# Attention followed by a SwiGLU block: batch-1 loads behind the casts of batch 0, transposes ahead of the second score burst, and the x of a batch read half a step later

## Chip, cores and metric

The kernel runs on one core of one Trainium2 chip. The metric is the device time of one execution in microseconds (us), as the median of several runs; lower is better.

## What is computed

The input is q, k, v of shape (8, 8, 576, 64) in fp32 (batch, heads, rows, width), 16 beacon rows of k and v per head that stand ahead of the others, and three weights of a gated block. Cut to its core, the reference is:

```
k_all = concatenate([beacon_k, k], axis=2);  v_all = concatenate([beacon_v, v], axis=2)
scores = (1 / sqrt(D)) * q @ k_all^T          # causal among the 576 rows, beacons always seen
a = softmax(scores);  attn = a @ v_all        # (8, 8, 576, 64)
x = attn.transpose(0, 2, 1, 3).reshape(4608, 512)
g = x @ w_gate;  val = x @ w_val              # 512 -> 1536
out = (g * sigmoid(g) * val) @ w_out          # 1536 -> 512, fp32
```

## The kernel before

The recording order is written by hand: instructions stand on each engine in the order in which the text calls them, and an engine takes them in that order. Waits are derived from it: an instruction that reads a tile waits for the last write of the same region that stands ahead of it in the text, and a write waits for the reads ahead of it.

**Attention** goes by batch b and head pair m (4 pairs). For a pair, `cast_k` and `cast_q` (L167 to L178) turn the fp32 tiles `k32` and `q32` into bf16 (`kb`, `qb`), `transpose_k` and `transpose_q` (L180 to L192) transpose them on TensorE into a PSUM tile `t_ps`, which VectorE copies to `kT` and `qT`. `scores1` and `scores2` (L215 to L254) are the two score bursts of a pair: matmuls into two PSUM tiles `s_ps`, Exp on ScalarE into the tiles `p`, causal masks with `affine_select` on GpSimd (L238, two behind the first burst, four behind the second), and then the next group of `pool_todo`: DMA issues on GpSimd's queue for v, the weights, and the k and q of batch 2 onwards. `pv(b, m, hh)` (L258) multiplies with v for one head into `pv_ps` and VectorE normalises into `x` (L274, L275).

**The gated block** goes by chunks of 512 tokens. `G()` runs one unit: eight matmuls of 512 columns (L307), a Tanh (L316) and two VectorE passes (L318, L321) that leave one of the 12 slices of `hT`. `gq` is the queue of units. `F(n)` takes n matmuls of `out_steps` (L326) from the queue `fq`; 12 of them fill one output tile, which VectorE copies out (L345) and SyncE's queue stores. The input `xT` of batch 0 comes from TensorE transposes (`x_transpose_pair`, L282); that of batches 1 to 7 from DMA transposes of `x`, five per batch, on SyncE's queue (`x_transpose`, L290 to L295). A chunk ends at a multiple of 512, a batch at a multiple of 576, so the units of chunk b-1 need the first few of the five blocks of batch b-1.

PSUM: `big` has three buffers (score tiles and units share them), `att` and `outp` have one each. `att` holds in turn `pv_ps`, `xt_ps` and, from batch 1 on, `t_ps`.

**The start** (L374 to L382): SyncE's and ScalarE's queues load k32 and q32 of batch 0, pair by pair. Behind them, on SyncE's queue, stand the 24 loads of batch 1 into the same tiles (L377), in the text ahead of every cast. So the casts of batch 0 wait for those loads too, and read what they left: the scores of batch 0 are computed from the q and k of batch 1.

**Batch 0** (L401 to L417) does for each pair: `scores1`, the first half of the previous pair's `pv`, `scores2`, the second half, an x transpose, then casts and transposes of the next pair (`prep`), all of which stand behind the second burst.

**Steps from batch 1 on** (L430 to L471): a step is one pair. From batch 2 on it has three units: one ahead of `scores1`, one behind `scores2`, one at the end; in batch 1 two. In the step m == 1 the units of chunk b-1 are put into `gq` behind `scores2` and ahead of the second unit:

```python
        if m == 1 and b > 1:
            gq += [(b - 1, f) for f in range(NF)]
            fq += out_steps(b - 2, one_bank)
        if units:
            G()
        if prev:
            pv(*prev, 1)
        F(6)
        if m == 0 and b > 1:
            x_transpose(b - 1)
        if units > 1:
            G()
```

So `x_transpose` is issued at the end of step m == 0, and its result is first read by the second unit of step m == 1.

Of the kernel before, what the change touches and what calls it, by code (L numbers as in the profile page):

```python
# [24 lines left out]
NPE = 3  # L25
# [21 lines left out]
def kernel(  # L47
# [12 lines left out]
    nc = tc.nc  # L60
# [6 lines left out]
    NF = DFF // P  # L67
# [12 lines left out]
    att = ctx.enter_context(tc.tile_pool(name="att", bufs=1, space=bass.MemoryType.PSUM))  # L80
    outp = ctx.enter_context(tc.tile_pool(name="outp", bufs=1, space=bass.MemoryType.PSUM))
# [20 lines left out]
    def tiles(t):  # L102
        return t[:].rearrange("p (c h d) -> p c h d", c=NKT, h=H)
# [14 lines left out]
    def load_q_f32(eng, b, h0, h1):  # L118
        spans(eng, tiles(q32), q, b, h0, h1, 0, 4, 0)
        rows(eng, tiles(q32), q, b, h0, h1, 4, 0, 512, 64)  # L120

    def load_k_f32(eng, b, h0, h1):
        d = tiles(k32)
        rows(eng, d, beacon_k, b, h0, h1, 0, 0, 0, NB)
        rows(eng, d, k, b, h0, h1, 0, NB, 0, P - NB)
        spans(eng, d, k, b, h0, h1, 1, 4, P - NB)
        rows(eng, d, k, b, h0, h1, 4, 0, 496, 80)
# [39 lines left out]
    def cast_k(b, m):  # L167
        d, t, h = tiles(kb[b % 2]), tiles(k32), slice(2 * m, 2 * m + 2)
        nc.vector.tensor_copy(d[:, 0:4, h, :], t[:, 0:4, h, :])  # L169
        nc.vector.tensor_copy(d[0:80, 4, h, :], t[0:80, 4, h, :])  # L170

    def cast_q(b, m):
        d, t, h = tiles(qb[b % 2]), tiles(q32), slice(2 * m, 2 * m + 2)
        for o, i in ((d[:, 0:4, h, :], t[:, 0:4, h, :]), (d[0:64, 4, h, :], t[0:64, 4, h, :])):
            if b:
                nc.scalar.activation(o, i, ACT.Copy)
            else:
                nc.vector.tensor_copy(o, i)  # L178
# [9 lines left out]
    def transpose_k(b, m, pool, tag):  # L188
        transpose_pair(kT, kb, 80, b, m, pool, tag)

    def transpose_q(b, m, pool, tag):
        transpose_pair(qT, qb, 64, b, m, pool, tag)  # L192

    def prep(b, m):
        cast_k(b, m)
        cast_q(b, m)
        transpose_k(b, m, outp, "outp")
        transpose_q(b, m, outp, "outp")

    def dma_transposes(b):  # L200
        def one(dst, src, c, n):
            nc.sync.dma_start_transpose(
# [47 lines left out]
    def scores1(b, m):  # L250
        scores(b, m, 0, SCORES1, P1_COLS)

    def scores2(b, m):
        scores(b, m, 1, SCORES2, P2_COLS)  # L254
# [27 lines left out]
    def x_transpose_pair(b, m):  # L282
        t_ps = att.tile([P, S], BF16, name="xt_ps", tag="att")
        for c, (q0, n) in enumerate(QBLOCKS):
            nc.tensor.transpose(
                t_ps[:, q0 : q0 + n], xs[b][0:n, c, P * m : P * m + P], ident[0:n, 0:n]
            )
        nc.vector.tensor_copy(xT[:, m, S * b : S * b + S], t_ps[:])
# [63 lines left out]
    gq, fq = [], []  # L352
# [3 lines left out]
    def G():  # L356
        if gq:
            return gv_unit(*gq.pop(0))
# [15 lines left out]
    for h in range(0, H, 2):  # L374
        load_k_f32(nc.sync, 0, h, h + 2)
        load_q_f32(nc.scalar if h < 4 else nc.sync, 0, h, h + 2)
    for h in (0, 4):  # L377
        load_k_f32(nc.sync, 1, h, h + 4)
        load_q_f32(nc.sync, 1, h, h + 4)
    make_identity(nc, ident)  # L380
    for load in v_loads(0, 0, 4) + v_loads(0, 4, 8):
        load()  # L382
# [15 lines left out]
    def after(s):  # L398
        return steps[s + 1] if s + 1 < len(steps) else (B, 0)

    prep(0, 0)  # L401
    last = NPAIR - 1
    for m in range(NPAIR):
        scores1(0, m)
        if m:
            pv(0, m - 1, 0)
        scores2(0, m)
        if m:
            pv(0, m - 1, 1)
        if m >= 2:  # L410
            x_transpose_pair(0, m - 2)
        if m < last:
            prep(0, m + 1)
    x_transpose_pair(0, last - 1)
    pv(0, last, 0)
    pv(0, last, 1)
# [13 lines left out]
    for s in range(NPAIR, len(steps)):  # L430
        b, m = steps[s]
        nxt = after(s)
        units = {NPAIR: 0, NPAIR + 1: 2, NPAIR + 2: 2, NPAIR + 3: 2}.get(s, 3)
        if units > 2:
            G()
        scores1(b, m)
        if nxt[0] == 1:
            cast_k(*nxt)
        if prev:
            pv(*prev, 0)  # L440
        F(6)
        scores2(b, m)
        if nxt[0] == 1:
            cast_q(*nxt)
        if nxt[0] < NPE:
            transpose_k(*nxt, att, "att")
        if m == 1 and b > 1:
            gq += [(b - 1, f) for f in range(NF)]
            fq += out_steps(b - 2, one_bank)
        if units:  # L450
            G()
        if prev:
            pv(*prev, 1)
        F(6)
        if m == 0 and b > 1:
            x_transpose(b - 1)
        if units > 1:
            G()
        if nxt[0] < NPE:
            transpose_q(*nxt, att, "att")  # L460

        if m == 1 and NPE <= b + 1 < B:
            todo = dma_transposes(b + 1)
        for _ in range(4):
            if todo:
                todo.pop(0)()
        if m == 3 and NPE <= b + 2 < B:
            pool_todo += group(k_loads(b + 2, 0, H) + q_loads(b + 2, 0, H), 6)
        if m == 1 and NPE <= b + 1 < B:
            pool_todo += group(v_loads(b + 1, 0, H), 3)  # L470
        prev = (b, m)  # L471
# [51 lines left out]
```

## Time and profile before

| | us |
|---|---|
| median of 3 runs (460.53 to 462.31) | 461.3 |
| the profiled execution | 461.59 |
| its span, first to last instruction | 459.9 |
| TensorE (PE) busy with matmuls | 390.9 (85%) |
| VectorE (DVE) busy | 232.8 |
| ScalarE (ACT) busy | 172.3 |
| GpSimd (POOL) busy, its DMA issues among it | 178.4 |
| mean granted TensorE clock | 0.948 of full speed |

In the rows below, a line of the timeline gives start, length, engine, source line, operation, tile written and tiles read, how many instructions are merged, and in brackets the idle time of the engine ahead of it and what ended it. SPq and ACTq are DMA issues on the queues of SyncE and ScalarE. "PEclk" is the granted clock. The 1.7 us between span and time lie outside the span.

### The profile page before, as it was taken

The page shows a single profiled execution, that of the slowest core. Times are in us where ns is not written, and L with a number is a line of the kernel's source. Part 1 is how long each engine was busy: PE and PEld are TensorE (multiplying, and loading weights), DVE is VectorE, ACT ScalarE, POOL GpSimd, SP SyncE. Part 2 cuts the span into 40 slices and gives each one's busy share as a digit, 9 for nine tenths or more (in the row PEclk, how much of TensorE's full clock was granted, in tenths as well). Part 3 has the DMA queues.
Part 4 walks back from the last instruction along what each step waited for, and adds up shares of the span by engine and source line. Part 5 has one row for each costly group of instructions (what it writes and reads, how often), then busy time and mean ns, then how long its engine had stood idle before and what let it go on. Part 6 is the DMA issues. An engine that isn't in the chain of part 4 may idle for free.

```text
span 459.9 us, 7296 instructions
## 1 busy us (share of the span) xinstructions
PE 390.9 (85%) x2780; PEld 186.1 (40%) x2780; DVE 232.8 (51%) x450; ACT 172.3 (37%) x245; POOL 178.4 (39%) x345
## 2 busy tenths in 40 slices
PE   0056697777799959998999799999999998999996
PEld 0034444343344424443444344444444443444442
DVE  1035444555256525654555365656655664576562
ACT  1034227444344434444444344445455421222220
POOL 7038608765861733456436442646222100000000
PEclk9999578889799979998999899999999999999999
DMA  9969658669999991959497949899221013010002
GB/s 165 173 134 99 73 87 95 45 50 164 140 143 90 88 161 29 132 53 171 66 115 70 178 64 109 73 173 121 42 76 47 23 34 87 26 46 20 27 30 108
DMA packets 169491, 41.70 MB, mean 91 GB/s; under 512 B 159216, under 2 KB 164848, under 8 KB 169456
## 3 DMA queue, kind: packets, MB, share of 16 engines
q0 software_dynamic: 101936, 16.75, 51.1%
q1 hardware_dynamic: 65120, 23.89, 25.9%
q10 hardware_dynamic: 2400, 0.59, 0.6%
q8 instruction: 22, 0.36, 0.3%
q14 instruction: 13, 0.11, 0.1%
HBM read 38.27 MB, written 9.44 MB: 104 GB/s over the span
## 4 chain that ended last, share of the span: by engine, by line
PE 65%; DVE 13%; DMA 9%; ACT 5%; SPq 4%; issue 2%; POOL 1%; DVEq 0%; ACTq 0%
PE gv_ps L307 32%; PE o_ps L336 18%; PE pv_ps L266 7%; PE s_ps L220 7%; DMA xT<-x 5%; DVE u L318 4%; DVE hT L321 4%; ACT th L316 4%; SPq L295 2%; DMA k<-in_k_dram 2%; PE t_ps L185 2%; DMA q<-in_q_dram 2%; DMA vb<-in_v_dram 1%; DVE x L275 1%; SPq L108 1%
## 5 line engine op out<-in xcount | busy, mean ns | idle before, releaser
L318 DVE SCALAR_TENSOR_TENSOR u<-th,gv_ps 128x512 f32<-128x512 f32 x108 | 74.3, 688 | 148.5 <-ACT th L316 147.8
L316 ACT ACTIVATE th<-gv_ps 128x512 f32<-128x512 f32 x108 | 64.5, 597 | 202.9 <-PE gv_ps L307 197.6
L238 POOL TENSOR_SCALAR_AFFINE_SELECT p<-p 128x256 bf16<-128x256 bf16 x192 | 66.7, 379 | 186.2 <-ACT p L229 185.8
L229 ACT ACTIVATE p<-s_ps 128x720 bf16<-128x720 f32 (+1 forms) x128 | 103.7, 868 | 64.6 <-PE s_ps L220 64.4
L307 PE MATMUL gv_ps<-xT,wg 128*128 128x512 bf16 x432 | 117.3, 396 | 9.8 <-DMA xT<-x 9.8
L307 PE MATMUL gv_ps<-xT,wv 128*128 128x512 bf16 x432 | 114.4, 388 | 0.0
L336 PE MATMUL o_ps<-wo,hT 128*128 128x512 bf16 x432 | 105.6, 382 | 2.1 <-DVE o_sb L345 2.1
L321 DVE SCALAR_TENSOR_TENSOR hT<-gv_ps,u 128x512 bf16<-128x512 f32 x108 | 74.7, 691 | 3.7
L307 PEld LDWEIGHTS <-wv 128*128 128x128 bf16 x432 | 43.3, 100 | 54.4 <-issue 6.3
L307 PEld LDWEIGHTS <-wg 128*128 128x128 bf16 x432 | 40.9, 101 | 58.1 <-issue 15.4
L220 PE MATMUL s_ps<-qT,kT 64*128 64x80 bf16 (+5 forms) x384 | 47.7, 308 | 12.1 <-DVE qT L186 7.4
L336 PEld LDWEIGHTS <-hT 128*128 128x128 bf16 x432 | 39.3, 99 | 42.8 <-issue 3.7
L266 PEld LDWEIGHTS <-p 128*128 128x128 bf16 x960 | 39.2, 103 | 25.6 <-issue 15.0
L266 PE MATMUL pv_ps<-vb,p 128*128 128x65 bf16 x960 | 44.9, 203 | 4.0 <-DMA vb<-in_v_dram 2.4
L114 POOL DMA_DIRECT2D vb<-in_v_dram x50 | 39.9, 814 | 0.2 <-issue 0.2
L220 PEld LDWEIGHTS <-kT 64*128 64x128 bf16 x384 | 16.4, 99 | 43.5 <-issue 37.1
L275 DVE TENSOR_TENSOR x<-pv_ps,rec 128x320 bf16<-128x320 f32 x64 | 31.5, 492 | 2.2
L345 DVE COPY o_sb<-o_ps 128x512 f32<-128x512 f32 x36 | 24.8, 689 | 12.6 <-PE o_ps L336 12.1
L114 POOL DMA_DIRECT2D qb<-in_q_dram x35 | 28.6, 853 | 0.0
L185 PE MATMUL t_ps<-ident,kb 128*128 128x128 bf16 (+1 forms) x60 | 7.1, 265 | 25.0 <-DVE kb L169 23.8
L114 POOL DMA_DIRECT2D kb<-in_k_dram x35 | 28.4, 833 | 0.0
L274 DVE RECIPROCAL rec<-pv_ps 128x5 f32<-128x5 f32 x64 | 11.9, 186 | 19.5 <-PE pv_ps L266 19.5
(30 smaller groups left out, 67.0 us busy)
## 6 DMA issues: line engine op xcount, KB each, us to landing
out_dram<-o_sb SPq DMA_DIRECT2D x36, 256.0 KB, 2.2
qb<-in_q_dram POOLq DMA_DIRECT2D x20, 128.0 KB, 5.3
vb<-in_v_dram POOLq DMA_DIRECT2D x18, 128.0 KB, 5.9
kb<-in_k_dram POOLq DMA_DIRECT2D x15, 128.0 KB, 4.1
k<-in_k_dram SPq DMA_DIRECT2D x16, 96.0 KB, 2.8
q<-in_q_dram SPq DMA_DIRECT2D x12, 128.0 KB, 2.8
wg<-in_moe_w_gate_dram POOLq DMA_DIRECT2D x4, 384.0 KB, 5.5
wv<-in_moe_w_val_dram POOLq DMA_DIRECT2D x4, 384.0 KB, 6.7
```

What stands on the lines that cost most here:

```text
L114: eng.dma_start(dst[p0 : p0 + n, c, h0:h1, 0:D], src[b, h0:h1, r : r + n, :].rearrange("h j d -> j h d"))
L220: nc.tensor.matmul(s[hh][:, col : col + n], lhsT=kT[b % 2][r, m, P * t : P * t + P], rhs=qT[b % 2][r, m, q0 : q0 + n], start=True, stop=True,)
L229: nc.scalar.activation(p[:, cols[0] : cols[1]], s[hh][:, cols[0] : cols[1]], ACT.Exp, scale=0.125)
L238: nc.gpsimd.affine_select(out=ap, in_=ap, compare_op=ALU.is_ge, fill=0.0, base=base, pattern=pattern, channel_multiplier=-1,)
L266: nc.tensor.matmul(o_ps[:, c, 0 : D + 1], lhsT=pt[2 * (m % 2) + hh][w][:, col : col + P], rhs=vb[b % 2][:, t, h, 0 : D + 1], start=(t == 0 ...
L275: nc.vector.tensor_tensor(out=xs[b][:, :, D * h : D * h + D], in0=o_ps[:, :, 0:D], in1=rec[:].to_broadcast([P, NKT, D]), op=ALU.mult,)
L307: nc.tensor.matmul(ps[:, TOK * half : TOK * half + TOK], lhsT=w[:, kk, P * f : P * f + P], rhs=xT[:, kk, r : r + TOK], start=(kk == 0), st ...
L316: tanh = nc.scalar.activation(th[:], ps[:, 0:TOK], ACT.Tanh, scale=0.5)
L318: nc.vector.scalar_tensor_tensor(out=u[:], in0=th[:], scalar=1.0, in1=ps[:, 0:TOK], op0=ALU.add, op1=ALU.mult)
L321: nc.vector.scalar_tensor_tensor(out=hTs[j][:, f, :], in0=ps[:, TOK:1024], scalar=0.5, in1=u[:], op0=ALU.mult, op1=ALU.mult)
L336: nc.tensor.matmul(st["o"][:], lhsT=hTs[j][:, f, P * i : P * i + P], rhs=wo[:, f, :], start=(f == 0), stop=(f == NF - 1),)
L345: nc.vector.tensor_copy(o_sb[:], st["o"][:])
```

## The change

It has three parts. First, the batch-1 loads of k32 and q32 leave the start and are issued from the loop over batch 0, twelve behind pair 0 and twelve behind pair 1, behind the casts whose tiles they overwrite. Second, the casts of the next pair are done one pair earlier, its transposes stand between the two score bursts instead of behind the second, the x transpose of batch 0 stands right behind `scores1`, and in batch 1 (`units < 3`) `transpose_q` stands ahead of the second unit. Third, in step m == 1 the units of chunk b-1 are queued behind the second unit, so that the third one is the first to read the new `xT`; the second takes the last unit of the chunk before.

```diff
-    def prep(b, m):
-        cast_k(b, m)
-        cast_q(b, m)
-        transpose_k(b, m, outp, "outp")
-        transpose_q(b, m, outp, "outp")
...
-    for h in (0, 4):
-        load_k_f32(nc.sync, 1, h, h + 4)
-        load_q_f32(nc.sync, 1, h, h + 4)
...
-    prep(0, 0)
     last = NPAIR - 1
+    cast_k(0, 0)
+    cast_q(0, 0)
+    transpose_k(0, 0, outp, "outp")
+    transpose_q(0, 0, att, "att")
+    cast_k(0, 1)
+    cast_q(0, 1)
     for m in range(NPAIR):
         scores1(0, m)
+        if m >= 2:
+            x_transpose_pair(0, m - 2)
+        if m < last:
+            transpose_k(0, m + 1, outp, "outp")
         if m:
             pv(0, m - 1, 0)
+        if m < last:
+            transpose_q(0, m + 1, outp, "outp")
         scores2(0, m)
         if m:
             pv(0, m - 1, 1)
-        if m >= 2:
-            x_transpose_pair(0, m - 2)
-        if m < last:
-            prep(0, m + 1)
+        if m + 1 < last:
+            cast_k(0, m + 2)
+            cast_q(0, m + 2)
+        if m in (0, 1):
+            load_k_f32(nc.sync, 1, 4 * m, 4 * m + 4)
+            load_q_f32(nc.sync, 1, 4 * m, 4 * m + 4)
...
         if nxt[0] < NPE:
             transpose_k(*nxt, att, "att")
+        if units:
+            G()
         if m == 1 and b > 1:
-            gq += [(b - 1, f) for f in range(NF)]
             fq += out_steps(b - 2, one_bank)
-        if units:
+        if units < 3 and nxt[0] < NPE:
+            transpose_q(*nxt, att, "att")
+        if units == 2:
             G()
         if prev:
             pv(*prev, 1)
         F(6)
         if m == 0 and b > 1:
             x_transpose(b - 1)
-        if units > 1:
+        if m == 1 and b > 1:
+            gq += [(b - 1, f) for f in range(NF)]
+        if units > 2:
             G()
-        if nxt[0] < NPE:
-            transpose_q(*nxt, att, "att")
+            if nxt[0] < NPE:
+                transpose_q(*nxt, att, "att")
```

How this moves instructions, at three places. The first is VectorE's start, its first casts (`k_89` and `q_88` are the fp32 tiles, `kb_92` and `qb_90` the bf16 ones of batch 0; the names in brackets are the semaphores waited for, DMAHW those of loads on SyncE's and ScalarE's queues). Before:

```order
L169 CAST kb_92<-k_89 128x4x128 [waits DMAHW2_49,DMAHW3_49,DMAHW1_49,DMAHW0_49]
L170 CAST kb_92<-k_89 80x128 [waits DMAHW6_49]
L178 CAST qb_90<-q_88 128x4x128 [waits DMAHW7_49,DMAHW0_49]
L178 CAST qb_90<-q_88 64x128 [waits DMAHW5_49,DMAHW3_49]
L186 COPY kT_98<-t_ps 128x592 [waits PE_49]
```

and now:

```order
L169 CAST kb_92<-k_89 128x4x128 [waits DMAHW4_49,DMAHW6_49,DMAHW2_49,DMAHW1_49]
L170 CAST kb_92<-k_89 80x128 [waits DMAHW0_49]
L178 CAST qb_90<-q_88 128x4x128 [waits DMAHW3_49]
L178 CAST qb_90<-q_88 64x128 [waits DMAHW5_49]
L186 COPY kT_98<-t_ps 128x592 [waits PE_49]
```

The casts wait for other loads than before: those of pair 0 of batch 0, the first on the queues. On SyncE's queue the loads of batch 1 keep their place, behind all loads of batch 0 and ahead of the first x transpose; six of them now also wait for VectorE (its casts).

The second place is VectorE's list in batch 0 from the transposes of pair 1 on. Before:

```order
L186 COPY qT_96<-t_ps 128x576
L274 RECIPROCAL rec<-pv_ps 128x5
L275 TENSOR_TENSOR x<-pv_ps,rec 128x5x64
L274 RECIPROCAL rec<-pv_ps 128x5
L275 TENSOR_TENSOR x<-pv_ps,rec 128x5x64
L169 CAST kb_92<-k_89 128x4x128
L170 CAST kb_92<-k_89 80x128
L178 CAST qb_90<-q_88 128x4x128
L178 CAST qb_90<-q_88 64x128
L186 COPY kT_98<-t_ps 128x592
```

and now:

```order
L186 COPY qT_96<-t_ps 128x576
L169 CAST kb_92<-k_89 128x4x128
L170 CAST kb_92<-k_89 80x128
L178 CAST qb_90<-q_88 128x4x128
L178 CAST qb_90<-q_88 64x128
L186 COPY kT_98<-t_ps 128x592
L268 RECIPROCAL rec<-pv_ps 128x5
L269 TENSOR_TENSOR x<-pv_ps,rec 128x5x64
L186 COPY qT_96<-t_ps 128x576
L268 RECIPROCAL rec<-pv_ps 128x5
L269 TENSOR_TENSOR x<-pv_ps,rec 128x5x64
```

The casts of pair 2 stand ahead of both normalisations of pair 0, and the copies to `kT` and `qT` lie among them instead of behind.

The third place is VectorE's list in a step of batch 1 (`kT_99`, `qT_97` are those of batch 1, `hT` and `u` belong to units). Before:

```order
L186 COPY kT_99<-t_ps 128x592
L318 SCALAR_TENSOR_TENSOR u<-th,gv_ps 128x512
L321 SCALAR_TENSOR_TENSOR hT<-gv_ps,u 128x512
L274 RECIPROCAL rec<-pv_ps 128x5
L275 TENSOR_TENSOR x<-pv_ps,rec 128x5x64
L318 SCALAR_TENSOR_TENSOR u<-th,gv_ps 128x512
L321 SCALAR_TENSOR_TENSOR hT<-gv_ps,u 128x512
L186 COPY qT_97<-t_ps 128x576
```

and now:

```order
L186 COPY kT_99<-t_ps 128x592
L312 SCALAR_TENSOR_TENSOR u<-th,gv_ps 128x512
L315 SCALAR_TENSOR_TENSOR hT<-gv_ps,u 128x512
L186 COPY qT_97<-t_ps 128x576
L312 SCALAR_TENSOR_TENSOR u<-th,gv_ps 128x512
L315 SCALAR_TENSOR_TENSOR hT<-gv_ps,u 128x512
L268 RECIPROCAL rec<-pv_ps 128x5
L269 TENSOR_TENSOR x<-pv_ps,rec 128x5x64
```

The copy to `qT` moves ahead of the second unit's two passes, the normalisation of the second head behind them. The third part of the change moves no instruction from batch 3 on, because units look alike; there is one unit fewer in step m == 1 of batch 2 and one more behind the last step.

## Rows read from the trace of the kernel before

**Rows 1.** Waits of the whole span: engine, line waited for: us, times, longest.

```profile
DVE kb L169 <- DMA k<-in_k_dram: 17.7, 1, 17.7
DVE kb L170 <- DMA k<-in_k_dram: 1.3, 1, 1.3
DVE qb L178 <- DMA q<-in_q_dram: 1.7, 2, 1.0
PE gv_ps L307 <- DMA xT<-x: 9.8, 4, 4.7
PE pv_ps L266 <- DMA vb<-in_v_dram: 2.4, 1, 2.4
PE o_ps L336 <- DVE o_sb L345: 2.1, 1, 2.1
```

**Rows 2.** Timeline, 0 to 28 us: start, length, instruction, idle ahead.

```profile
3.44 0.33 SPq L114 DMA_DIRECT2D k<-in_k_dram  x1
...
17.68 2.08 SPq L108 DMA_DIRECT2D k<-in_k_dram  x4
...
20.97 0.43 DVE L169 CAST kb<-k 128x512 bf16<-128x512 f32 x1 [17.66 <-DMA k<-in_k_dram]
...
27.06 1.24 PE L220 MATMUL s_ps<-qT,kT 64*128 64x496 bf16 x5 [0.55 <-DVE qT L186]
```

**Rows 3.** Chain that ended last, 0 to 62 us: start, length, piece.

```profile
2.21 3.65 DMA k<-in_k_dram
...
10.63 4.87 DMA q<-in_q_dram
```

**Rows 4.** Busy time by stretch: from:to length, then each engine, PEclk, DMA, GB/s.

```profile
27.06:59.67 32.61, 21.52 (x218) 14.01 (x218) 13.13 (x37) 12.64 (x16) 21.28 (x42) 0.81 0.81 100
59.67:104.73 45.06, 36.72 (x272) 18.04 (x270) 22.79 (x49) 20.92 (x33) 26.44 (x50) 0.83 0.69 66
```

**Rows 5.** Timeline of POOL, 27 to 60 us.

```profile
29.10 0.40 POOL L238 TENSOR_SCALAR_AFFINE_SELECT p<-p 128x256 bf16<-128x256 bf16 x1 [19.17 <-ACT p L229]
...
31.86 0.76 POOL L154 DMA_DIRECT2D wg<-in_moe_w_gate_dram  x1
...
38.90 2.14 POOL L114 DMA_DIRECT2D vb<-in_v_dram  x3
...
45.26 1.74 POOL L238 TENSOR_SCALAR_AFFINE_SELECT p<-p 128x256 bf16<-128x256 bf16 x4
...
53.42 1.22 POOL L238 TENSOR_SCALAR_AFFINE_SELECT p<-p 128x256 bf16<-128x256 bf16 x4
```

**Rows 6.** Timeline of PE, 73 to 95 us, two steps of batch 1.

```profile
82.20 0.52 PE L185 MATMUL t_ps<-ident,qb 128*128 128x128 bf16 x5 [0.68 <-ACT th L316]
84.02 0.58 PE L220 MATMUL s_ps<-qT,kT 64*128 64x496 bf16 x4 [1.30 <-DVE qT L186]
...
94.11 0.58 PE L220 MATMUL s_ps<-qT,kT 64*128 64x496 bf16 x4 [1.31 <-DVE qT L186]
```

**Rows 7.** Busy time by stretch, step m == 1 of batches 3 to 7.

```profile
160.09:177.75 17.66, 12.91 (x80) 5.64 (x80) 6.02 (x12) 5.05 (x7) 5.12 (x10) 0.81 1.09 112
208.57:222.46 13.89, 11.89 (x80) 5.42 (x80) 6.02 (x12) 5.05 (x7) 5.29 (x10) 0.88 1.42 146
253.28:267.86 14.58, 11.65 (x80) 5.02 (x80) 6.01 (x12) 5.06 (x7) 5.28 (x10) 0.88 1.27 146
298.67:309.40 10.73, 10.23 (x79) 4.71 (x79) 6.02 (x12) 5.05 (x7) 5.50 (x11) 1.00 1.81 164
340.22:350.49 10.27, 10.18 (x80) 4.71 (x80) 6.01 (x12) 5.05 (x7) 2.08 (x6) 1.00 0.27 72
```

**Rows 8.** Timeline of PE in such steps, around the units.

```profile
168.05 1.86 PE L307 MATMUL gv_ps<-xT,wg 128*128 128x512 bf16 x4 [4.66 <-DMA xT<-x]
...
343.46 1.04 PE L307 MATMUL gv_ps<-xT,wg 128*128 128x512 bf16 x4
...
346.94 1.03 PE L307 MATMUL gv_ps<-xT,wg 128*128 128x512 bf16 x4
```

## Prediction

> **What bounds the kernel now.** I read the waits first, for idle time that is on the path [rows 1]. VectorE's first cast waits 17.7 us for k loads, with nothing else running; TensorE waits 9.8 us in four places for the transposed x, 2.4 us for v of batch 2, 2.1 us for an output tile. The timeline of the start shows why the first wait is long: the last k load of pair 0 is issued at 3.44, but the cast starts at 20.97, behind the loads issued from 17.68 on, those of batch 1 [rows 2]. Busy time by stretch then splits the span. Batch 0 (27.06 to 59.67) keeps TensorE busy for 21.5 of 32.6 us at a mean clock of 0.81, batch 1 (59.67 to 104.73) for 36.7 of 45.1 us at 0.83 [rows 4]. Late steps are full: 10.18 of 10.27 us, clock 1.00 [rows 7]. So the end is set by TensorE's work from batch 2 on, and by everything that keeps TensorE waiting ahead of it. All three parts of the change act on such waits.
>
> **1. The start.** Removed: the wait of the first casts for 24 loads. What is left is pair 0's own loads. One issued at 2.21 landed 3.65 us later; others later on took up to 4.87 [rows 3]. The last one of pair 0, issued at 3.44, so lands between 7.1 and 8.3; I take 7.2, since it sees what the load at 2.21 saw. From the first cast to the first scores it took 27.06 - 20.97 = 6.1 us, of which 1.3 + 1.7 were waits for late pieces [rows 1, 2], so 3.1 us are work, and part of that (the main cast and four transposes) runs before the last piece lands. I put the first scores at 9.8; bounds are 9.5 and 8.3 + 3.1 = 11.4. **Gain 17.3 us (15.7 to 17.6).**
>
> **2. Batch 0.** Before, 32.6 us from first scores to first unit [rows 4], because each pair's casts, transposes and copies stand between its predecessor's last `pv` and its own scores. Now they lie between the bursts, and GpSimd becomes the bound. From its first mask to its last it has, for four pairs, two masks of 0.4 and four masks that take 1.22 to 1.74 (say 1.4), 4 x 2.2 = 8.8 us; two weight loads ahead of the last mask, twice 2 x 0.76 = 3.0 us; four groups of v issues, about 2.1 each, 8.4 us [rows 5]. That is 20.2 us. The first mask comes 2.0 us behind the first scores (29.10 against 27.06) [rows 2, 5], and pair 0's second burst now waits for pair 1's two transposes and copies, some 2.2 us more on GpSimd. The last mask ends 24.4 us behind the first scores; two `pv` with their normalisations and a transpose follow, 59.67 less 54.64 or 5.0 us before [rows 4, 5], 1.2 less now because an x transpose no longer stands ahead of them. First unit at 24.4 + 3.8 = 28.2 us, or 38.0 on the clock. **Gain 4.4 us (1 to 7)**: down to 1 if loads are late, up to 7 if the masks overlap better than I count.
>
> The 24 loads themselves cost nothing. Their large ones go out from about 17.7 on as before [rows 2], behind batch 0's, since the casts that the first twelve wait for are done by then; the last twelve wait for pair 3's cast, at about 22, so with 24 issues of about 0.5 (2.08 for four) and at most 4.87 to land [rows 2, 3] all are there before batch 1 reads them at about 41. Nothing stands behind them on SyncE's queue until the first x transpose. Casts one pair earlier wait on VectorE for loads: a q load of pair 2, issued at 10.63, landed at 15.5 [rows 3], the small one behind it perhaps at 16.1, and what is queued behind these casts (a copy to `kT`) is needed at about 16.5.
>
> **3. Batch 1.** In a step of 10.1 us (94.11 less 84.02), `transpose_q` waits 0.68, and the next scores wait 1.30 for its copy [rows 6]. Both go. But the second head's normalisation now stands behind the second unit's two passes, so the next `pv` waits for it. Followed by hand through the queues, the first of three such steps lets the scores start 1.5 us earlier but holds the `pv` behind them until the normalisation is done, so that it gains only 0.2; in the other two the hold is there at both ends of the step and what stays is the removed 1.30 each; less idle time should give back some slow clock, 0.5 in all. **Gain 3.3 us (-0.5 to 6).**
>
> **4. The shifted unit.** Step m == 1 of batch 2 has one unit fewer: twice four matmuls of 1.04 that overlap [rows 8], 1.7 us. The v wait in that step, 2.4 now [rows 1], grows by up to 1.4, since the step ahead of its loads is shorter; I take 0.7. The unit comes back behind the last step, where TensorE waits 2.1 us for an output copy [rows 1]: that copy is now covered, net 0.35 gained. **Gain 1.4 us (0 to 3.3).**
>
> **5. The x wait.** A step m == 1 without a wait takes 10.27 us; batches 3 to 6 took 17.66, 13.89, 14.58 and 10.73 [rows 7], together 15.8 us too much. Of it 9.8 are idle [rows 1], the other 6.0 slow matmuls behind the idle time: after a wait of 4.66, four took 1.86 against 1.04 [rows 8], at the lower of the clock's two levels (1.2 GHz instead of 2.4). The first reader moves from the second unit to the third, 346.94 - 343.46 = 3.48 us later [rows 8]. That covers all but the first wait, of which 1.2 us stay, and with some slow clock 2.0. **Gain 13.8 us (10.5 to 15.8).** What hides it is the chunk's last unit, half a `pv` and six output matmuls; if the DMA transposes land later than before, the wait returns.
>
> **Sum.** 17.3 + 4.4 + 3.3 + 1.4 + 13.8 = 40.2 us off the profiled execution's 461.59 gives 421.4. The median of the runs is 0.3 lower, so **421 us**.
>
> **The rivals.**
>
> *Loads bound batch 0* (0.10). Batch 0 moved 100 GB/s with DMA busy for 0.81 of the time [rows 4]; now the same loads are pressed into a shorter stretch. For: GpSimd's v and weight loads now run beside batch 1's k and q. Against: it was not busy all the time, and the first unit needs only the first weights. If the first unit came at 48 instead of 38, the time is 431.
>
> *Casts hold GpSimd* (0.07). In rows, four masks took 1.74 us while VectorE was casting and 1.22 while it was not [rows 5], 0.5 us more; three v issues took 2.14, some 0.7 each, like the weight issues at 0.76. A pair's two large casts are 0.43 each [rows 2], the two small ones about half, 1.3 us together. If they stopped GpSimd's masks and issues for their whole length, three pairs would add 3.9 us to the stage that GpSimd bounds: 425. The Trainium skill, page "SBUF — State Buffer", section "SBUF: two separate sides", says just this: while VectorE runs an fp32 SBUF-to-SBUF copy, GpSimd cannot write the descriptors of its own DMAs. The masks agree with it in part; the issues in this trace do not show it.
>
> *The x wait moves along* (0.06). x is transposed later relative to its reader, or its transposes land 2 to 3 us later among denser loads. The gain of part 5 falls to 5: 430.
>
> *The casts still wait for the whole tile* (0.02). Then only parts 3 to 5 and a little of 2 are left: 440. Against: the casts name other semaphores now.
>
> *Slower* (0.02). Denser work could keep TensorE at a lower mean clock in the long stretch from 129 to 444, which shows 1.00 in undisturbed steps [rows 7]. 315 us at a mean clock c take 315/c; at c = 0.89 the 40 us are gone, at 0.85 the time is 477. Against: the late steps are already full and hold 1.00.
>
> **How the numbers follow.** The forecast has 0.73, its own range being 413 to 430 from the bounds above, not all at one end. With loads, casts and x wait included the range is **412 to 432**. A measurement of this kernel tells about 0.5% from no change. Faster by more than that: all but the last rival and odd mishaps, 0.97; same 0.01; slower 0.02.
>
> **What would show it.** First cast at 6 to 7.5 us, first scores near 10, first unit near 38, with GpSimd nearly full in between; steps of batch 1 at about 9 us; no wait for xT above 2 us, steps m == 1 of batches 4 to 7 at 10.3; no wait for an output copy near the end. I am wrong on the start if the first cast comes later than 9, on batch 0 if TensorE waits there for DMA or GpSimd is idle, on part 5 if two or more waits for xT remain.

## The result, and the profile after

| | before | changed |
|---|---|---|
| median of the runs, us | 460.91 (4 runs, 459.47 to 462.31) | 422.6 (4 runs, 420.83 to 423.44) |
| ratio, 95% interval | | 0.9164 (0.9123 to 0.9205) |
| the profiled execution | 461.59 | 420.83 |
| its span | 459.9 | 419.1 |

The kernel became 8.4% faster; forecast were 421 us, in a range of 412 to 432. A second measurement of the same two kernels gave 422.93 us and 0.9179 (0.913 to 0.9228).

First the page of the changed kernel: busy time of each engine, share of the span, instructions.

```profile
PE 379.7 (91%) x2780; PEld 181.2 (43%) x2780; DVE 233.1 (56%) x450; ACT 172.8 (41%) x245; POOL 178.3 (43%) x345
```

The other engines do what they did before. TensorE's busy time falls by 11.2 us, from 390.9, with the same matmuls; the mean granted clock was 0.948 before and is 0.967 now. The remaining 29.6 us of the span are idle time of TensorE that is gone.

The waits of the whole span, in the columns of [rows 1]:

```profile
DVE kb L169 <- DMA k<-in_k_dram: 4.4, 2, 2.4
...
PE pv_ps L260 <- DVE x L269: 4.1, 4, 1.4
...
PE pv_ps L260 <- DMA vb<-in_v_dram: 2.2, 3, 1.8
...
PE gv_ps L301 <- DMA xT<-x: 1.4, 1, 1.4
...
PE o_ps L330 <- DVE o_sb L339: 0.4, 1, 0.4
```

Against [rows 1]: the first cast waits 2.4 us instead of 17.7; TensorE waits for the transposed x once, 1.4 us, instead of four times, 9.8; for an output copy 0.4 instead of 2.1; for v about as long as before. Grown is the wait of `pv` for a normalisation of `x`: four times, 4.1 us, two of them in batch 0 and two in batch 1; before it was one of 0.8 us.

The start in the timeline of the changed kernel, to be read beside [rows 2], and behind it the first wait of batch 0, for the k of pair 1:

```profile
5.68 0.43 DVE L169 CAST kb<-k 128x512 bf16<-128x512 f32 x1 [2.38 <-DMA k<-in_k_dram]
...
8.77 0.98 PE L214 MATMUL s_ps<-qT,kT 64*128 64x496 bf16 x4 [0.55 <-DVE qT L186]
...
10.72 0.43 DVE L169 CAST kb<-k 128x512 bf16<-128x512 f32 x1 [2.01 <-DMA k<-in_k_dram]
...
11.21 0.68 PE L185 MATMUL t_ps<-ident,kb 128*128 128x128 bf16 x5 [1.46 <-DVE kb L169]
```

Busy time by stretch, in the columns of [rows 4]: batch 0, batch 1, the steps m == 0 and 1 of batch 2, the next three, the step m == 1 of batch 3, and the end, from the step m == 2 of batch 7 on.

```profile
8.77:37.16 28.39, 19.13 (x219) 12.28 (x218) 13.57 (x37) 13.05 (x16) 22.50 (x44) 0.80 1.46 182
37.16:79.58 42.42, 33.49 (x271) 16.73 (x268) 22.75 (x49) 21.10 (x33) 26.44 (x50) 0.89 0.91 100
79.58:102.52 22.94, 16.85 (x143) 8.71 (x142) 9.87 (x21) 9.16 (x13) 17.59 (x29) 0.85 1.69 150
102.52:133.53 31.01, 30.60 (x244) 14.60 (x244) 18.44 (x35) 14.89 (x21) 16.55 (x32) 1.00 1.35 111
133.53:145.35 11.82, 10.34 (x79) 4.63 (x79) 6.01 (x12) 5.05 (x7) 5.10 (x10) 1.00 1.53 167
309.73:419.10 109.37, 104.80 (x573) 48.07 (x572) 62.44 (x99) 27.42 (x43) 4.14 (x12) 1.00 0.13 45
```

and two stretches of the kernel before that [rows 4] doesn't have, the steps m == 0 and 1 of batch 2 and the end:

```profile
104.73:129.07 24.34, 18.41 (x151) 9.25 (x151) 11.02 (x22) 9.76 (x14) 17.62 (x29) 0.86 1.68 148
350.49:459.90 109.41, 103.07 (x565) 47.29 (x564) 61.09 (x97) 26.83 (x42) 4.16 (x12) 1.00 0.13 45
```

Set against the same stretches of before (in us, the first scores of a step being its start):

| stretch | before | changed | gain | forecast |
|---|---|---|---|---|
| to the first scores | 27.06 | 8.77 | 18.29 | 17.3 |
| batch 0, to the first unit | 32.61 | 28.39 | 4.22 | 4.4 |
| batch 1, to the scores of batch 2 | 45.06 | 42.42 | 2.64 | 3.3 |
| steps m == 0 and 1 of batch 2 | 24.34 | 22.94 | 1.40 | 1.0 |
| the next three steps | 31.02 | 31.01 | 0.01 | 0 |
| from there to the end of step m == 1 of batch 7 | 190.40 | 176.20 | 14.20 | 13.8 |
| the end | 109.41 | 109.37 | 0.04 | 0.35 |

The gains add to 40.80 us, the difference of the spans. They are of one profile each. Other profiles below have the same instructions in some of these stretches, and there a stretch early in the kernel differs by one to two microseconds from profile to profile.

### The profile page after: what moved, and what is told of

Its sections match the earlier page's. It is cut to its first block, busy times and chain, and to the rows that moved or that the text cites. A ratio compares the mean times of both kernels' runs of the same rounds, so it can differ in the third digit from the quotient of the medians.

```text
span 419.1 us, 7309 instructions
## 1 busy us (share of the span) xinstructions
PE 379.7 (91%) x2780; PEld 181.2 (43%) x2780; DVE 233.1 (56%) x450; ACT 172.8 (41%) x245; POOL 178.3 (43%) x345
## 4 chain that ended last, share of the span: by engine, by line
PE 69%; DVE 12%; DMA 8%; ACT 5%; issue 2%; SPq 1%; POOL 1%; ACTq 0%; DVEq 0%
PE gv_ps L301 33%; PE o_ps L330 21%; PE pv_ps L260 7%; PE s_ps L214 6%; DVE u L312 5%; DVE hT L315 4%; DMA q<-in_q_dram 4%; ACT th L310 4%; PE t_ps L185 2%; DMA xT<-x 2%; DMA vb<-in_v_dram 1%; DMA k<-in_k_dram 1%; SPq L289 1%; POOL vb L114 1%; DVE x L269 1%
## 5 line engine op out<-in xcount | busy, mean ns | idle before, releaser
L301 PE MATMUL gv_ps<-xT,wg 128*128 128x512 bf16 x432 | 112.9, 384 | 1.4 <-DMA xT<-x 1.4
L301 PE MATMUL gv_ps<-xT,wv 128*128 128x512 bf16 x432 | 111.5, 381 | 0.0
L301 PEld LDWEIGHTS <-wg 128*128 128x128 bf16 x432 | 39.9, 99 | 47.8 <-issue 3.0
L260 PE MATMUL pv_ps<-vb,p 128*128 128x65 bf16 x960 | 43.7, 199 | 11.1 <-DVE x L269 4.1
L214 PE MATMUL s_ps<-qT,kT 64*128 64x80 bf16 (+5 forms) x384 | 45.8, 302 | 7.4 <-DVE qT L186 3.1
L260 PEld LDWEIGHTS <-p 128*128 128x128 bf16 x960 | 38.2, 101 | 30.7 <-issue 18.8
L214 PEld LDWEIGHTS <-kT 64*128 64x128 bf16 x384 | 15.0, 98 | 37.3 <-issue 32.0
```

What stands on the lines that cost most here:

```text
L214: nc.tensor.matmul(s[hh][:, col : col + n], lhsT=kT[b % 2][r, m, P * t : P * t + P], rhs=qT[b % 2][r, m, q0 : q0 + n], start=True, stop=True,)
L260: nc.tensor.matmul(o_ps[:, c, 0 : D + 1], lhsT=pt[2 * (m % 2) + hh][w][:, col : col + P], rhs=vb[b % 2][:, t, h, 0 : D + 1], start=(t == 0 ...
L301: nc.tensor.matmul(ps[:, TOK * half : TOK * half + TOK], lhsT=w[:, kk, P * f : P * f + P], rhs=xT[:, kk, r : r + TOK], start=(kk == 0), st ...
```

## The experiments

The ratios are to the kernel before, on the same chip. Three profiles of kernels with the changed kernel's own code in batch 0 gave 28.39, 28.09 and 29.31 us for that stretch, so a difference of a microsecond there, in one profile, is not more than such profiles differ by themselves. "The stretch" below is this one, from first scores to first unit.

**The three parts apart.** The first two runs add one part to the kernel before. Only the batch-1 loads are moved:

```diff
-    for h in (0, 4):
-        load_k_f32(nc.sync, 1, h, h + 4)
-        load_q_f32(nc.sync, 1, h, h + 4)
...
             prep(0, m + 1)
+        if m in (0, 2):
+            load_k_f32(nc.sync, 1, 2 * m, 2 * m + 4)
+            load_q_f32(nc.sync, 1, 2 * m, 2 * m + 4)
```

> Only the batch-1 loads are moved behind the casts of batch 0 (twelve behind pair 0, twelve behind pair 2, since here the casts come later); transposes and units stay as in the kernel before. Theory (the parts act on separate stretches and add up): first scores near 8.8 instead of 27.1, the stretch from there to the first unit stays near 32.6, the rest unchanged: about 18 us faster, 443. Rival (loads bound batch 0): the first scores come early, but the stretch grows to 40 or more, since the same bytes are pressed together: 6 to 10 us faster, 451 to 455.

Measured: 444.06 us, ratio 0.9599 (0.9557 to 0.9641), about 18.5 us. The first cast began at 6.87, the first scores at 10.01; batch 0 took 32.91 (32.61 before).

Only the units of a chunk are queued later:

```diff
-        if m == 1 and b > 1:
-            gq += [(b - 1, f) for f in range(NF)]
-            fq += out_steps(b - 2, one_bank)
         if units:
             G()
+        if m == 1 and b > 1:
+            fq += out_steps(b - 2, one_bank)
...
             x_transpose(b - 1)
+        if m == 1 and b > 1:
+            gq += [(b - 1, f) for f in range(NF)]
```

> Only the new units are queued half a step later. Theory: the steps m == 1 of batches 3 to 6 lose 15.8 us above 10.27 before and about 1.5 now, the step of batch 2 one unit, the tail gives it back: 14 to 16 us faster, 446. Rival (the x wait is set by how crowded the DMA engines are, and without the earlier start they are as crowded as before): two or more waits for xT stay, 5 to 10 us faster, 451 to 456.

Measured: 448.32 us, ratio 0.9721 (0.9686 to 0.9755), about 12.9 us, less than the 14 to 16 expected. From the step m == 1 of batch 3 to the end of that of batch 7 it took 176.33 us (176.20 in the changed kernel, 190.40 before), so the x waits gave what they should; what is missing lies ahead of them, where batch 1 took 46.55 us with the code of the kernel before (45.06 there). The wait for the transposed x, in the waits of this run:

```profile
PE gv_ps L307 <- DMA xT<-x: 1.5, 1, 1.5
```

The third run is the changed kernel with the loads back at the start and the units queued at the old place, so that only the order of casts and transposes is new. Like the kernel before, it computes the scores of batch 0 from the q and k of batch 1.

> Only the order of casts and transposes in batches 0 and 1 is the new one; the loads of batch 1 stand at the start as before and the units are queued as before. Theory: batch 0 shrinks from 32.6 to about 28.4, batch 1 from 45.1 to about 42.5: 6 to 7 us faster, 454. Rival (the new order pays only where loads arrive one by one): below 3 us faster, 458 or more.

Measured: 452.34 us, ratio 0.9805 (0.9768 to 0.9842), about 9.0 us, more than the 6 to 7 expected; batch 0 took 26.61, batch 1 took 43.12. The parts alone give 18.5 + 12.9 + 9.0 = 40.4 us, the whole 38.6 (8.36% of 461.6). Each of the three is uncertain by 1.6 to 1.9 us, so the difference of 1.8 is not clear of noise: within it, the parts add. In one stretch they do touch: batch 0 took 26.61 us where its loads were all there before it began, and 28.39 in the changed kernel.

**What bounds batch 0.** The forecast had said: GpSimd. GpSimd's timeline in the changed kernel, with the `pv` of TensorE that waits for the last masks:

```profile
14.82 1.53 POOL L232 TENSOR_SCALAR_AFFINE_SELECT p<-p 128x256 bf16<-128x256 bf16 x4 [2.72 <-ACT p L223]
16.31 0.76 POOL L154 DMA_DIRECT2D wg<-in_moe_w_gate_dram  x1
...
20.52 1.64 POOL L232 TENSOR_SCALAR_AFFINE_SELECT p<-p 128x256 bf16<-128x256 bf16 x4
...
25.86 1.46 POOL L114 DMA_DIRECT2D vb<-in_v_dram  x2 [0.36 <-DMA wv<-in_moe_w_val_dram]
...
32.84 1.22 POOL L232 TENSOR_SCALAR_AFFINE_SELECT p<-p 128x256 bf16<-128x256 bf16 x4
...
33.33 0.73 PE L260 MATMUL pv_ps<-vb,p 128*128 128x65 bf16 x10 [0.83 <-POOL p L232]
```

From the second masks of pair 0, at 14.82, to the last masks, at 32.84, GpSimd has no idle time but the 0.36 us ahead of a v issue, and TensorE then waits 0.83 us for those masks (in the whole stretch 1.5). So GpSimd's list is the chain through this stretch, as forecast; the runs that follow test it. The first experiment takes the 24 masks of batch 0 out:

```diff
-            for ap, pattern, base in selects:
+            for ap, pattern, base in selects if b else []:
```

> The changed kernel without the 24 causal masks of batch 0 on GpSimd (so batch 0 is computed unmasked). Theory (GpSimd's list bounds batch 0): some 9 us of its 20 us list go, the stretch from first scores to first unit falls from 28.4 to 24 or less, and the time by 4 to 5. Rival (the chain TensorE, VectorE, PSUM buffer bounds it, GpSimd is full beside it): the stretch falls by no more than the 1.5 to 3 us that TensorE waits for masks there, to 25.5 to 27.

Measured: 425.8 us in one run, and a stretch of 29.61 us, no shorter than with masks; neither the theory nor the rival had this. GpSimd's queue and VectorE's cast of q of pair 2 in the run without masks:

```profile
10.05 0.79 POOL L154 DMA_DIRECT2D wg<-in_moe_w_gate_dram  x1
...
12.37 3.60 POOL L114 DMA_DIRECT2D vb<-in_v_dram  x5
...
18.47 0.43 DVE L178 CAST qb<-q 128x512 bf16<-128x512 f32 x1 [3.83 <-DMA q<-in_q_dram]
```

Without masks nothing holds GpSimd's list back, and its loads go out early: the first weights at 10.05 instead of 16.31, and five v loads by 16. The q loads of pairs 2 and 3 that are issued on SyncE's queue in the same time land later. Their view, issues from 9 to 17 us, first in the changed kernel (six), then in the run without masks (four):

```profile
DMA to landing us min/median/max: 2.4/3.4/4.4
```

```profile
DMA to landing us min/median/max: 4.3/7.8/8.0
```

The cast of pair 2 then waits 3.83 us for q, and all behind it is late. So the experiment took away one thing and added another, and says nothing about the bound: the masks were what spaced GpSimd's loads out. That the early loads are what slowed the q loads is the likely reading, since the edit moved nothing else; it was not tried by itself. A run that keeps the masks, but cuts them to 8 columns, so that each still waits for its Exp, is the cleaner one:

```diff
+            if b == 0:
+                selects = [(both[:, :, 0:8], [[0, 2], [1, 8]], 0)]
+                if which:
+                    selects.append((p[:, 416:424], [[1, 8]], -16))
```

> The changed kernel, with the 24 masks of batch 0 cut to 8 columns each (so batch 0 is masked only in part): they still wait for the Exp, but are short. Theory (GpSimd's list of 20 us bounds batch 0): the list loses 4 to 6 us and the stretch from first scores to first unit falls from 28.4 to 24 or less. Rival (the shared PSUM buffer and loads bound it, and leaving the masks out only let GpSimd's loads run ahead): it falls by the 1.5 us that TensorE waits for masks, to about 27, and pair 2's q loads land as in the changed kernel, within 1 us.

Measured: 418.99 us in one run, the stretch 26.60 us, 1.8 less than 28.39 (1.5 less than the shortest of the three profiles). That is near the 1.5 us that TensorE waits for masks in the changed kernel. It doesn't speak against GpSimd: its busy time in the stretch fell by 4.0 us (22.50 to 18.54), but its list from the second masks of pair 0 to the last masks only by 1.3 us (18.02 to 16.68), because in it GpSimd now stood idle for 1.7 us, 1.05 of it ahead of the same v issue. And TensorE's waits for the masks of pairs 2 and 3 did not go: they were 0.71 and 0.83 us and are 1.22 and 0.20. The profile puts the 1.22 down to a v load, but the v of batch 0 was issued before 11 us; this `pv` starts at 26.78, 0.30 us behind the start of pair 2's masks, as that of pair 3 starts 0.28 behind its own.

The third candidate is `att`, the one PSUM buffer that `pv`, its normalisation and the x transposes pass between TensorE and VectorE. With the second head's `pv` of batch 0 in `outp`:

```diff
-        o_ps = att.tile([P, NKT, 68], FP32, name="pv_ps", tag="att")
+        pool, tag = (outp, "outp") if b == 0 and hh else (att, "att")
+        o_ps = pool.tile([P, NKT, 68], FP32, name="pv_ps", tag=tag)
```

> The changed kernel, with the second head's pv of batch 0 in the PSUM buffer outp instead of att. Theory (the one buffer att, handed from TensorE to VectorE and back, bounds the end of batch 0: TensorE waits there 1.9 us for x, 1.8 for xT and 1.2 for x again): the stretch from first scores to first unit falls from 28.4 to 26 or 27, the time by 1.5 to 2.5 us. Rival (GpSimd's list): GpSimd's last mask ends at the same time, the stretch falls by 0.5 or less.

Measured: 423.29 us, ratio 0.9153 (0.9082 to 0.9224), the same as the changed kernel; the stretch took 27.07 us, the way from the first unit to the first scores of batch 1 9.11 instead of 8.12. With the last pair's `pv` left in `att` (`b == 0 and hh and m < 3`):

> The changed kernel with the second head's pv of batch 0 in the PSUM buffer outp for the first three pairs, and in att for the last. With outp for all four the stretch of batch 0 became 1.3 us shorter, but the way from the first unit to the first scores of batch 1 became 1.0 longer (9.11 against 8.12 us). Theory: that loss comes from the last pair's pv, which holds outp while the transposes and the first output matmuls behind it want it; with it in att the stretch is 27.1 us, the way behind it 8.1, and the time 1.3 below the changed kernel's on the same chip. Rival: the loss has another cause (the unit's weights or the passes behind it come no earlier), the way behind stays at 9 us or the stretch goes back to 28.4, and the time is within 0.5 us of the changed kernel's.

Measured: 422.87 us, ratio 0.9177 (0.9135 to 0.922); the stretch 28.35 us, the way behind it 8.23, as the rival had it. So what there was to gain lay in the last pair, and came back as loss right behind it, as far as differences of a microsecond in one profile each can tell. Beside it ran the changed kernel again:

> The changed kernel itself, once more, beside the kernel before on the same chip as the two other runs: a ratio near 0.916. It tells how much the ratio moves between chips, and is what the pv buffer of the first three pairs is compared with. If it moves by 0.003 or more, gains of about 1 us in single runs of other chips can't be read from the times, only from the stretches of the profile.

Measured: 422.93 us, ratio 0.9179 (0.913 to 0.9228). The second buffer is worth nothing that can be measured in the time. In this profile of the changed kernel the stretch took 29.31 us, and TensorE's waits at the masks of pairs 2 and 3 were 2.23 and 0.71 us. The first of them is put down to a v load here too, but that `pv` starts 0.49 us behind the start of the masks, as the one at 33.33 above does.

Then loads, masks and buffer together: the order alone (loads at the start, 26.61 us) with both of the last two edits.

> The changed kernel's order with the batch-1 loads back at their old place (so the casts of batch 0 find all their data there), the masks of batch 0 cut to 8 columns, and the second head's pv of batch 0 in the PSUM buffer outp. The cut masks leave out most of batch 0's causal masking. Looked at is the stretch from first scores to first unit, 28.39 us in the changed kernel, 26.61 with the loads landed alone. Theory: no single engine or queue bounds batch 0 after the change; loads (1.8 us), masks (1.8) and the handing over of att (1.3) are separate short waits on one chain, and add: 26.61 - 1.8 - 1.3 = 23.5 us, 23 to 24.3. Rival: the three lie beside each other, and taking one away lets another grow: 25.5 us or more. TensorE's own matmuls take 19.1 us of the stretch in the changed kernel, at a granted clock of 0.80; under both theories the clock stays below 0.9.

Measured: 447.21 us in one run (with the late start), and 22.08 us for batch 0. The stretch with loads in place, then with all three out, from the busy time by stretch of these two kernels:

```profile
26.35:52.96 26.61, 18.85 (x218) 12.24 (x219) 12.83 (x38) 12.95 (x16) 20.98 (x42) 0.83 0.96 118
```

```profile
27.04:49.12 22.08, 16.44 (x218) 10.57 (x219) 12.28 (x38) 13.06 (x16) 17.01 (x42) 0.95 1.05 126
```

That is below the theory's 23 to 24.3. GpSimd's timeline of the last run, from the second masks of pair 0 to the last masks, with TensorE's `pv` behind them:

```profile
31.41 1.01 POOL L236 TENSOR_SCALAR_AFFINE_SELECT p<-p 128x16 bf16<-128x16 bf16 x4 [1.29 <-ACT p L223]
...
46.02 0.66 POOL L236 TENSOR_SCALAR_AFFINE_SELECT p<-p 128x16 bf16<-128x16 bf16 x4
...
46.32 1.00 PE L265 MATMUL pv_ps<-vb,p 128*128 128x65 bf16 x25 [0.38 <-POOL p L236]
```

Between the two GpSimd's timeline shows no idle time, and TensorE waits for its last masks, though only 0.38 us. So the theory that no single engine bounds batch 0 does not hold: GpSimd's list does, here as in the changed kernel, with the next chain close behind. GpSimd's timelines cut the stretch in three: from the first scores to the second masks of pair 0, GpSimd's list from there to the start of the last masks, and from there to the first unit (us).

| kernel | to the second masks | GpSimd's list | to the first unit | stretch |
|---|---|---|---|---|
| changed | 6.05 | 18.02 | 4.32 | 28.39 |
| changed, second profile | 6.36 | 18.20 | 4.75 | 29.31 |
| loads in place | 4.37 | 17.49 | 4.75 | 26.61 |
| masks of 8 columns | 5.82 | 16.68 | 4.10 | 26.60 |
| second buffer for `pv` | 5.69 | 18.07 | 3.31 | 27.07 |
| all three | 4.37 | 14.61 | 3.10 | 22.08 |

The two profiles of the changed kernel differ by 0.2 to 0.4 us in each part, and each edit acts on one part by more than that: loads in place on the first (1.7 us), short masks on the list (1.3, and 2.9 with the loads in place), the buffer on what follows the last masks (1.0 and 1.7). With the loads in place the list is 2.9 us shorter and the rest 1.7: together the 4.5 us between 26.61 and 22.08. By TensorE's rows, 2.1 of them are idle time and 2.4 busy time, at a mean granted clock of 0.95 instead of 0.83. That the clock would stay under 0.9 was wrong, but the clock doesn't explain the busy time: in the run without masks it was 0.95 too, and the same 218 matmuls took 18.75 us.

**Batch 1.** The changed kernel's new wait is in TensorE's timeline of two steps:

```profile
60.50 0.58 PE L214 MATMUL s_ps<-qT,kT 64*128 64x496 bf16 x4
62.51 0.62 PE L260 MATMUL pv_ps<-vb,p 128*128 128x65 bf16 x15 [1.43 <-DVE x L269]
...
64.21 1.03 PE L301 MATMUL gv_ps<-xT,wg 128*128 128x512 bf16 x4
...
71.15 0.62 PE L260 MATMUL pv_ps<-vb,p 128*128 128x65 bf16 x15 [1.42 <-DVE x L269]
```

The scores wait for `qT` no more (1.30 and 1.31 in [rows 6]), but the `pv` behind them waits 1.43 and 1.42 for the normalisation, which stands on VectorE behind the second unit's two passes. To take this hold away, the second head's `pv` was put ahead of the second unit:

```diff
-        if units == 2:
-            G()
         if prev:
             pv(*prev, 1)
+        if units == 2:
+            G()
```

> The changed kernel, with the second head's pv of a batch-1 step put ahead of the second unit instead of behind it. Theory (in batch 1 the next pv waits for a normalisation that stands behind the second unit's two VectorE passes, 1.43 and 1.42 us in two steps): these waits go, the pv instead waits some 0.5 for the copy to qT; steps of batch 1 become 0.7 to 1.2 us shorter, the time falls by 1 to 3 us against the changed kernel. Rival (VectorE's order only moves the wait, the unit's passes then hold the next copy to kT): no change within 0.5 us.

Measured: 430.4 us, ratio 0.9305 (0.9248 to 0.9362), some 6 us slower than the changed kernel. TensorE's timeline of the step that took 13.30 us (8.64 in the changed kernel):

```profile
65.08 0.43 PE L185 MATMUL t_ps<-ident,kb 128*128 128x128 bf16 x5 [0.63 <-DVE x L269]
65.35 1.87 PE L301 MATMUL gv_ps<-xT,wg 128*128 128x512 bf16 x4
67.02 1.91 PE L301 MATMUL gv_ps<-xT,wv 128*128 128x512 bf16 x4
...
71.42 0.61 PE L260 MATMUL pv_ps<-vb,p 128*128 128x65 bf16 x15 [2.14 <-DVE qT L186]
71.87 1.57 PE L301 MATMUL gv_ps<-xT,wg 128*128 128x512 bf16 x4
```

The hold is gone, as the experiment meant, but `pv` needs `att`, and `att` is free only when VectorE has copied `qT`, which stands behind the first unit's Tanh and two passes: 2.14 us, three times (6.4 in all). The unit between `transpose_q` and `pv` had been the cover of this wait. And in this step four matmuls of a unit take 1.87 and 1.91 us instead of 1.03, the lower of the clock's two levels; in the step ahead of it, right behind the same wait of 2.14 us, they took 1.02. Neither the theory nor the rival had counted any of this. The last run joins this order, the second buffer, and `transpose_q` ahead of `pv` in all steps:

```diff
-        if units < 3 and nxt[0] < NPE:
+        if nxt[0] < NPE:
             transpose_q(*nxt, att, "att")
```

> The changed kernel with both of these orders, and transpose_q of batch 2 right behind the second unit as in batch 1 already. Theory: the gains add, and batch 2's waits of 1.4 us for qT go in two or three steps: 4 to 7 us faster than the changed kernel, 416 to 418. Rival (the loads of v and the weights set the pace, so an earlier batch 1 only waits longer for v of batch 2): 1 to 2 us faster.

Measured: 430.55 us, ratio 0.9328 (0.9257 to 0.9399); expected were 416 to 418. In its waits, the same mechanism:

```profile
PE pv_ps L261 <- DVE qT L186: 11.8, 7, 2.1
```

None of the runs that leave all masks in beats the changed kernel by more than they are uncertain.

## Why the prediction was right, and where it was not

**1. The start: right, gain 18.29 against 17.3.** The sum took 7.2 for the landing of pair 0's last loads and 2.6 us from there to the first scores. The cast of the large k piece could begin at 5.68, the small one followed at 6.83, and the scores came 1.94 us behind that, at 8.77 instead of 9.8: both terms were a little long. With the loads alone moved, the first cast began at 6.87 instead of 20.97. So the 17.7 us wait was the loads of batch 1, but for the few microseconds that pair 0's own loads take.

**2. Batch 0: right, with two terms that offset each other; 28.39 us against 28.2.** "GpSimd becomes the bound" is what the timelines show. From its first mask to its last GpSimd was busy for 19.89 of 23.26 us, where the sum had a list of 20.2. The last mask ended 25.29 us behind the first scores (forecast 24.4), and the first unit came 3.10 us behind it (forecast 3.8); that these two misses, 0.9 and 0.7, cancel is luck. The term that was wrong is the extra 2.2 us for pair 1's transposes and copies ahead of the second masks: GpSimd's idle time there was 2.72, but 1.07 with the loads in place. The other 1.7 us were pair 1's k, for which the cast waits 2.01 and the transposes behind it 1.46. The sum had loads at nothing; so the rival "loads bound batch 0" came true in a small part. What a faster GpSimd would give in the changed kernel was not tried; TensorE's waits at masks are 1.5 us in the first profile and 2.9 in the second.

The rival that casts hold GpSimd came true in its small half: four masks beside casts took 1.53 and 1.64 us against 1.22 without, 0.7 us together, not 3.9. Its other half is about the issues. The Trainium skill, page "SBUF — State Buffer", section "SBUF: two separate sides", says that GpSimd cannot write the descriptors of its DMAs while VectorE runs an fp32 copy within SBUF. The trace of the changed kernel doesn't show this: two v issues, the second of them beside the casts of pair 3 from 19.96 on, took 1.47 us, two with no cast beside them 1.46. In the run without masks one weight issue beside casts took 1.09 us instead of 0.76.

The 24 loads themselves cost nothing: none of VectorE's waits for k loads lies in batch 1 (the two in the table of waits start before 11 us). But the forecast's reason for it, that all have landed when batch 1 begins at about 41, did not hold: single issues took up to 4.04 us instead of 0.5, and the last q load, issued at 38.73, landed 9.0 us later. The pairs that read the last twelve are cast from 51 on.

**3. Batch 1: the hold was there, the size right; how the gain splits is open; 2.64 against 3.3.** "The next `pv` waits for it" is in the trace, with 1.43 and 1.42 us. Other profiles with the same instructions in batch 1 give the size better: 45.06, 46.66 and 46.55 us in three with the old order, 42.39 to 43.68 in eight with the new one, 3.1 us apart in the mean. The forecast took 2.8 us from idle time removed and 0.5 from clock. The rows of the first pair of profiles say otherwise: TensorE's idle time in batch 1 is 8.93 us now (42.42 less 33.49), and was 8.34 ([rows 4], 45.06 less 36.72); its busy time fell by 3.2, at a clock of 0.89 instead of 0.83. In these, then, the new waits replaced the removed ones in full, and the step of the forecast that failed is "what stays is the removed 1.30 each". But the gain is not the clock alone. The busy time of the three steps that begin in batch 1 with a unit behind their scores, in the first profile:

```profile
51.28:60.50 9.22, 8.91 (x68) 4.65 (x67) 3.55 (x9) 5.04 (x8) 8.57 (x16) 0.71 1.21 119
60.50:69.14 8.64, 6.51 (x71) 3.52 (x69) 5.54 (x13) 5.16 (x8) 7.09 (x15) 1.00 0.69 45
69.14:79.58 10.44, 8.22 (x79) 4.17 (x76) 6.52 (x14) 4.46 (x6) 6.95 (x13) 1.00 0.85 74
```

and the first two of them in the second profile of the same kernel:

```profile
52.28:60.82 8.54, 8.05 (x68) 4.49 (x69) 3.53 (x9) 5.04 (x8) 8.11 (x15) 0.77 1.35 135
60.82:70.63 9.81, 7.75 (x72) 4.17 (x70) 5.55 (x13) 5.16 (x8) 8.94 (x17) 0.83 0.76 49
```

Before, the three stood at 0.83 to 0.84, and took 9.93, 10.09 and 10.62 us. In the second profile batch 1 as a whole took 43.01 us at a clock of 0.83, as before the change, so of the 2.64 us an estimated 0.6 (43.01 less 42.42) came with the higher clock. How the rest divides between waits and matmuls these rows can't tell, since they hold 264 to 272 matmuls of the same program. Step by step the forecast had 0.2, 1.3 and 1.3, and 0.5 of clock; measured in the first profile are 0.71, 1.45 and 0.18, and 0.3 from the stretch ahead of them (14.12 against 14.42). That the sum came near is in part luck. The experiment that moved `pv` shows how much hangs on the place: it made the kernel 6 us slower.

**4. The shifted unit: right in sum, 1.40 + 0.04 against 1.4.** In batch 2 one unit fewer gave 1.40 us; 1.0 were expected. The v waits did not grow (2.2 against 2.4 us), as the forecast had allowed for. This stretch took 22.94 to 24.97 us in eight profiles with one unit fewer and 24.17 to 25.38 in four without; the means lie 1.0 apart. At the end the output wait fell from 2.1 to 0.4 us, and the unit that came back took all of it: 0.04 instead of 0.35.

**5. The x wait: right, 14.20 against 13.8.** One wait is left, 1.4 us, forecast were 1.2. The 0.8 us of slow clock behind it did not come; in TensorE's timeline of the step m == 1 of batch 3

```profile
141.81 1.02 PE L301 MATMUL gv_ps<-xT,wg 128*128 128x512 bf16 x4 [1.39 <-DMA xT<-x]
```

four matmuls take 1.02 us, where after 4.66 us of idle time they took 1.86 [rows 8]. From batch 4 on the steps m == 1 take 10.27 us, like all others: the wait did not move along. The shift alone gave the same stretch, 176.33 us, so this gain needs neither of the other parts.

## What to carry to other kernels

When an engine is cut down to see whether it is the bound, measure how much shorter its list became up to the instruction that is waited for: short masks took 4.0 us off GpSimd's busy time in a stretch, but 1.3 off its list up to the last masks, and 1.8 off the stretch, though GpSimd was the bound all along. Before moving work off a place, ask what it covers there; a unit that stood between a transpose and its reader hid 2.14 us per step. And before explaining a difference of a microsecond or two between two profiles, look at a second profile of the same kernel: it may differ by as much.

## What was unexpected of the hardware

- Less work made the stretch longer: with GpSimd's masks gone its loads went out 6 us earlier, and q loads on SyncE's queue landed in 7.8 us (median) instead of 3.4.
- The same matmuls behind the same wait ran at either level of the clock. Behind 1.43 us of idle time ahead of a `pv`, the first half of the next unit took 0.87 us in one profile of the changed kernel (64.21 to 65.08, in the timeline of two steps) and 1.66 us in the other:

```profile
64.90 0.63 PE L301 MATMUL gv_ps<-xT,wg 128*128 128x512 bf16 x1
...
66.56 1.03 PE L301 MATMUL gv_ps<-xT,wv 128*128 128x512 bf16 x4
```

- On SyncE's queue, four q loads of batch 1 took 6.01 us to issue, against 2.08 for four k loads in [rows 2]; one alone took 3.31. The DMA engines moved 182 GB/s in this stretch and 100 before; whether that is the cause was not tried. Neither VectorE nor ScalarE, which cast them, waited for any.

```profile
21.61 6.01 SPq L108 DMA_DIRECT2D q<-in_q_dram  x4
```
